# Decode step with gated attention and FFN: the FFN row added inside PSUM, the output copied to one row and stored as one descriptor, and a finer cut of the last weight load

## Chip, cores and metric

The kernel runs on one core of a Trainium2 chip. The metric is the time of one execution on the device in microseconds (us). A run stands for one execution; a comparison is made of several runs of both kernels on the same chip, and the verdict is "faster" or "slower" only beyond 2%. Times inside an execution are read from one profiled execution per kernel and count from the start of its span; the span is some 2 us shorter than the time. PSUM is the memory in which TensorE adds up its products. A transfer (DMA) is issued by an instruction on an engine's queue, moved by up to 16 DMA engines, and has landed when the last update of its semaphore comes; a descriptor is one contiguous run of bytes of it; for the small store each shows as one packet in the trace. The granted clock is the share of TensorE's full clock that the trace records.

## The reference

One token attends over a cache of 32768 positions (32 query heads, 8 key/value heads, head size 128, model width 512), beside a small SwiGLU network, and a scalar gate g mixes both:

```python
g = _sigmoid((x * gate_w).sum(-1, keepdims=True))
a = _A_ref(x, A_k_cache, A_v_cache, A_wq, A_wo)      # softmax(q k) v, then @ wo
b = _B_ref(x, B_w_gate, B_w_up, B_w_down)            # (silu(x w_gate) * (x w_up)) @ w_down
return g * a + (1 - g) * b                           # [1, 1, 512] bf16
```

Keys and values are 134 MB of the 148 MB that the kernel reads, so it is a streaming kernel.

## The kernel before

The sync engine (SP) issues all loads in one order; `wo` is the last, in four pieces with a semaphore each. At the very end it stores the result from four partitions:

```python
WO_CUT = (16, 8, 4, 4)
# ...
elif e[0] == "wo":
    src = A_wo.rearrange("(p j) n -> p j n", j=WOJ)
    j0 = 0
    for c, n in enumerate(WO_CUT):
        sp.dma_start(wo_v[:, j0 : j0 + n, :], src[:, j0 : j0 + n, :]).then_inc(sem_ldo[c], 16)
        j0 += n
# ...
sp.wait_ge(sem_res, 1)
sp.dma_start(out[0, 0, :].rearrange("(c n) -> c n", c=OC), res[0:128:32, :]).then_inc(sem_out, 16)
sp.wait_ge(sem_out, 16)
```

On TensorE (PE) the attention output, brought into 32 columns `O2`, is multiplied with `wo`: 32 steps j, each with four products of one row and 128 columns. The four go to PSUM partitions 0, 32, 64 and 96, so the output row lies in four pieces on four partitions:

```python
pe.wait_ge(sem_O2, 1)
j0 = 0
for c, n in enumerate(WO_CUT):
    pe.wait_ge(sem_ldo[c], 16)
    for j in range(j0, j0 + n):
        for oc in range(OC):                      # OC = 4
            ins = pe.matmul(ps_a[32 * oc : 32 * oc + 1, :], O2[:, j : j + 1],
                            wo_v[:, j, oc * 128 : (oc + 1) * 128],
                            start=(j == 0), stop=(j == WOJ - 1))
    j0 += n
ins.then_inc(sem_pe_a, 1)
```

VectorE (DVE) had computed `(1 - g) * b` about 60 us into the span, and at the end forms the mix in one instruction:

```python
dve.tensor_scalar(b_pre[:, :], ps_b, omg[:, 0:1], None, op0=ALU.mult).then_inc(sem_bpre, 1)
# ... 290 us later ...
dve.wait_ge(sem_pe_a, 1)
dve.scalar_tensor_tensor(res[:, :], ps_a, g_col[:, 0:1], b_pre[:, :], ALU.mult, ALU.add).then_inc(sem_res, 1)
```

## Time and profile before

| | before |
|---|---|
| time, median of 3 runs | 353.69 us (353.55 to 353.71) |
| span of the profiled run | 351.6 us |
| DMA engines busy with loads | 98.3% of the span |
| last piece of `wo` lands | 348.19 us |
| PE ends the last product | 349.03 us |
| store: start of its issue to the end of the span | 349.57 to 351.60, 2.03 us |

The landing is the last update of the load's semaphore in the trace. The page of the kernel before, with the busy share of the DMA engines and their GB/s in 40 slices of the span, and two of the DMA queues (packets, MB, share of 16 engines):

```profile
span 351.6 us, 6018 instructions
...
DMA  8999999999999999999999999999999999999994
GB/s 325 436 406 438 421 440 439 429 427 429 431 432 436 429 429 432 440 425 429 432 440 425 432 429 440 429 429 429 440 432 425 432 436 432 429 429 436 414 418 184
...
q1 hardware_dynamic: 5912, 148.12, 98.3%
q8 instruction: 7, 0.11, 0.1%
```

The DMA engines are at nine tenths or more from the second slice to the last but one. Nothing done faster on another engine in the middle can be seen in the time; only work after the last bytes counts.

The chain of waits of the kernel before, its end (start us, us, what):

```profile
308.15 38.86 DMA ring<-in_A_wo_dram
...
347.05 0.59 PE ps L579 x11
347.64 0.69 issue
348.34 0.71 PE ps L579 x18
...
349.19 0.35 DVE res L821
```

The timeline of the kernel before (start us, length us, engine, line, operation, out<-in, shapes, count, idle time before it):

```profile
343.83 0.19 DVE L817 CAST O<-ps 128x32 bf16<-128x32 f32 x1 [0.30 <-PE ps L570]
...
344.08 2.73 PE L579 MATMUL ps<-ring,O 128*1 128x128 bf16 x96 [0.28 <-DVE O L817]
...
347.05 0.59 PE L579 MATMUL ps<-ring,O 128*1 128x128 bf16 x14 [0.24 <-DMA ring<-in_A_wo_dram]
...
348.34 0.70 PE L579 MATMUL ps<-ring,O 128*1 128x128 bf16 x18 [0.69 <-issue]
349.19 0.35 DVE L821 SCALAR_TENSOR_TENSOR res<-ps,g_col,b_pre 128x128 bf16<-128x128 f32 x1 [5.17 <-PE ps L579]
349.57 0.63 SPq L355 DMA_DIRECT2D out_dram<-res  x1
```

One line of SP's waits (us in total, times, longest us):

```profile
SPq L249 <- DMA out_dram<-res: 1.0, 1, 1.0
```

After the last landing come 0.84 us to the end of PE, 0.54 us until SP has the result (one DVE instruction of 0.35), 0.63 us in which SP issues the store, the wait of 1.0 us for it, and 0.4 us more to the end of the span: 3.4 us in all.

### The profile page before, as it was taken

To read this page: it belongs to the slowest core of one execution; us is meant where nothing else is said; L and a number is where in the kernel's file an instruction comes from. 1 tells how busy PE (TensorE), PEld (TensorE's weight loads), DVE (VectorE), ACT (ScalarE), POOL (GpSimd) and SP (SyncE) were. 2 spreads that over 40 slices of the span, in tenths; PEclk is the share of its full clock that TensorE was granted. 3 is DMA by queue.
4 is the path that set the end of the run, shared out by engine and by line. 5 is a ranking of instruction groups with operands and counts; after the bars stand their busy time and mean duration, and the time that the engine had idled before them with its cause. 6 is when DMAs were issued, how large, how long until landed. Compare 5 with 4: busy or idle time off the path is not lost. (4 is left out here: it accounts for less than half of the span.)

```text
span 351.6 us, 6018 instructions
## 1 busy us (share of the span) xinstructions
PE 252.5 (72%) x2623; PEld 184.6 (53%) x2623; DVE 196.8 (56%) x367; ACT 17.6 (5%) x52; POOL 5.6 (2%) x22
## 2 busy tenths in 40 slices
PE   0159896978395957858495968768497929688755
PEld 0157884745282626546383838455474618475423
DVE  1329276958184845838283756648365917558211
ACT  1000001100100010000100010000100010000100
POOL 0200000000000000000000000000000000000000
PEclk9999679999789998989789698989779987969665
DMA  8999999999999999999999999999999999999994
GB/s 325 436 406 438 421 440 439 429 427 429 431 432 436 429 429 432 440 425 429 432 440 425 432 429 440 429 429 429 440 432 425 432 436 432 429 429 436 414 418 184
DMA packets 5924, 148.24 MB, mean 422 GB/s; under 512 B 666, under 2 KB 668, under 8 KB 924
## 3 DMA queue, kind: packets, MB, share of 16 engines
q1 hardware_dynamic: 5912, 148.12, 98.3%
q8 instruction: 7, 0.11, 0.1%
q14 instruction: 1, 0.01, 0.0%
q10 hardware_dynamic: 4, 0.00, 0.0%
HBM read 148.11 MB, written 0.00 MB: 421 GB/s over the span
## 5 line engine op out<-in xcount | busy, mean ns | idle before, releaser
L736 DVE COPY ktT<-ps 128x1024 bf16<-128x1024 bf16 x256 | 163.3, 685 | 95.5 <-PE ps L446 92.9
L446 PE MATMUL ps<-ident_f,ring 128*128 128x128 f32 x1024 | 158.2, 311 | 56.0 <-PEq L364 56.0
L446 PEld LDWEIGHTS ps<-ident_f,ring 128*128 128x128 f32 x1024 | 133.8, 161 | 89.8 <-issue 65.6
L460 PE MATMUL ps<-ktT,qc 128*32 128x512 bf16 x512 | 41.6, 402 | 15.2 <-DVE ktT L736 15.1
L510 PE MATMUL ps<-ring,ET 128*16 128x512 bf16 x512 | 33.6, 407 | 2.9 <-DMA ring<-in_A_v_cache_dram 2.9
L510 PEld LDWEIGHTS ps<-ring,ET 128*16 128x16 bf16 x512 | 13.3, 92 | 19.3 <-DMA ring<-in_A_v_cache_dram 3.8
L460 PEld LDWEIGHTS ps<-ktT,qc 128*32 128x32 bf16 x512 | 7.9, 95 | 28.1 <-DVE ktT L736 24.3
L741 DVE TENSOR_REDUCE pmaxf<-ps 128x1 f32<-128x512 f32 x16 | 11.1, 692 | 13.7 <-DVEq L740 13.7
L525 PEld LDWEIGHTS ps<-osel,pv_sb 128*128 128x128 f32 x72 | 11.6, 244 | 3.0 <-issue 3.0
L525 PE MATMUL ps<-osel,pv_sb 128*128 128x4 f32 x72 | 11.3, 281 | 1.8 <-PEq L364 1.8
L598 ACT ACTIVATE qc<-qz 128x112 bf16<-128x112 bf16 x8 | 2.4, 296 | 198.6 <-DVE nbias L759 186.5
L614 ACT ACTIVATE P<-ps,nbias 128x512 bf16<-128x512 f32 x16 | 10.7, 675 | 30.2 <-DVE nbias L759 30.1
L772 DVE COPY pv_sb<-ps 128x512 f32<-128x512 f32 x9 | 6.1, 682 | 6.1 <-PE ps L510 6.1
L390 PE MATMUL ps<-xT,ring 128*128 128x1 bf16 x128 | 3.6, 165 | 6.7 <-PEq L364 6.7
L306 POOL PARTITION_ALL_REDUCE gmax<-pmax x8 | 3.0, 372 | 307.4 <-DVE pmax L748 307.4
L492 PE MATMUL ps<-ident,P 128*128 128x128 bf16 x64 | 6.2, 219 | 1.9 <-ACT P L614 1.4
L766 DVE COPY ET<-ps 128x512 bf16<-128x512 bf16 x16 | 6.7, 416 | 1.3 <-PE ps L492 1.3
L415 PEld LDWEIGHTS ps<-xT,ring 128*128 128x128 bf16 x112 | 6.8, 159 | 0.4 <-issue 0.4
L390 PEld LDWEIGHTS ps<-xT,ring 128*128 128x128 bf16 x128 | 3.5, 104 | 6.7 <-issue 6.7
L415 PE MATMUL ps<-xT,ring 128*128 128x1 bf16 x112 | 6.9, 198 | 0.0
L373 PE MATMUL ps<-ones_bf,x_row 1*128 1x1 bf16 x4 | 0.3, 171 | 8.5 <-DMA gw_row<-in_gate_w_dram 8.5
L492 PEld LDWEIGHTS ps<-ident,P 128*128 128x128 bf16 x64 | 4.8, 98 | 2.8 <-ACT P L614 1.9
(71 smaller groups left out, 36.9 us busy)
## 6 DMA issues: line engine op xcount, KB each, us to landing
ring<-in_A_k_cache_dram SPq DMA_DIRECT2D x16, 4096.0 KB, 24.9
ring<-in_A_v_cache_dram SPq DMA_DIRECT2D x15, 4096.0 KB, 32.5
ring<-in_A_wq_dram SPq DMA_DIRECT2D x1, 4096.0 KB, 12.6
ring<-in_A_v_cache_dram SPq DMA_DIRECT2D x2, 2048.0 KB, 29.4
ring<-in_A_wo_dram SPq DMA_DIRECT2D x1, 2048.0 KB, 36.0
ring<-in_B_w_gate_dram SPq DMA_DIRECT2D x1, 1792.0 KB, 26.7
ring<-in_B_w_up_dram SPq DMA_DIRECT2D x1, 1792.0 KB, 30.6
ring<-in_B_w_down_dram SPq DMA_DIRECT2D x1, 1792.0 KB, 43.5
```

What stands on the lines that cost most here:

```text
L390: ins = pe.matmul(ps_m[:, M_Q0 + h : M_Q0 + h + 1], wq_v[:, c, h * DH : (h + 1) * DH], xT[:, c : c + 1], start=(c == 0), stop=(c == KC - 1),)
L415: ins = pe.matmul(ps_m[:, base + j : base + j + 1], wt[:, c, :].rearrange("d (p j) -> d j p", j=FC)[:, j, :], xT[:, c : c + 1], start=(c = ...
L446: ins = pe.transpose(stb[:, t * 64 : (t + 2) * 64], two.bitcast(FP32), ident_f[:, :])
L460: ins = pe.matmul(ps_sc[hf][32 * c : 32 * c + 32, :], qc[:, e, 24 - PB * i : 56 - PB * i], kt[:, e, :], start=(i == 0 and e == 0), stop=(i ...
L492: ins = pe.transpose(ps_pt[:, hf * 512 + m * 128 : hf * 512 + (m + 1) * 128], P[:, hf, m * 128 : (m + 1) * 128], ident[:, :],)
L510: ins = pe.matmul(ps_pv[32 * c : 32 * c + 2 * PB, :], ET[:, hf, col : col + 2 * PB], src[:, i0 : i0 + 2, c, 2 * m : 2 * m + 2, :].rearrang ...
L525: ins = pe.matmul(ps_m[:, M_OT : M_OT + HPG], pv_sb[:, r * DH : (r + 1) * DH], osel[:, r * HPG : (r + 1) * HPG], start=(r == 0), stop=(r = ...
L614: act.activation(P[:, hf, :], ps_sc[hf], ACT.Exp, bias=nbias[:, 0:1], scale=SCALE, accum_out=esum[:, g, hf : hf + 1],).then_inc(sem_exp, 1)
L736: dve.tensor_copy(ktT[:, q % NKT, :], pst[q % NST]).then_inc(sem_cp, 1)
L741: ins = dve.tensor_reduce(pmaxf[:, hf : hf + 1], ps_sc[hf], AX.X, ALU.max)
L766: dve.tensor_copy(ET[:, hf, :], ps_pt[:, hf * 512 : (hf + 1) * 512]).then_inc(sem_ptc, 1)
L772: dve.tensor_copy(pv_sb[:, :], ps_pv).then_inc(sem_pvc, 1)
```

## The change

Its intent is to shorten this tail. The gate is folded into the softmax's denominator (`rSg`), and `(1 - g) * b` is written to one row and added inside PSUM by four products of a single 1 by 1 weight, so that nothing is left after `wo` but a copy. The four pieces are copied to one partition, two by ScalarE (ACT) and two by DVE, so that the store is one descriptor of 1 KB. And `wo` ends in pieces of 2 steps, so that only 8 products are left after the last landing in place of 16. The core of the diff:

```diff
-    WO_CUT = (16, 8, 4, 4)
+    WO_CUT = (16, 8, 4, 2, 2)
@@ SP
-                sp.wait_ge(sem_res, 1)
+                sp.wait_ge(sem_res, OC)
                 sp.dma_start(
-                    out[0, 0, :].rearrange("(c n) -> c n", c=OC), res[0:128:32, :]
+                    out[0, :, :], row[0:1, :]
                 ).then_inc(sem_out, 16)
@@ PE, before the products with wo (ps_a moves from bank 7 to bank 1)
+                for c in range(OC):
+                    pe.matmul(
+                        ps_a[32 * c : 32 * c + 1, :], ones_f[0:1, 0:1],
+                        b_row[0:1, c * 128 : (c + 1) * 128], start=True, stop=False,
+                    )
@@
-                                start=(j == 0),
+                                start=False,
@@ ACT, at the end
+                act.wait_ge(sem_pe_a, 1)
+                for c in range(2):
+                    act.activation(
+                        row[0:1, c * 128 : (c + 1) * 128], ps_a[32 * c : 32 * c + 1, :], ACT.Copy
+                    ).then_inc(sem_res, 1)
@@ DVE, about 60 us into the span: b_pre in one instruction becomes b_row in four
@@ DVE, after the softmax sums
+                dchain(dve.tensor_scalar(rSg[:, :], rS[:, :], g_col[:, 0:1], None, op0=ALU.mult))
@@ DVE, at the end
-                dve.scalar_tensor_tensor(res[:, :], ps_a, g_col[:, 0:1], b_pre[:, :], ALU.mult, ALU.add)
+                for c in range(2, OC):
+                    dve.tensor_copy(
+                        row[0:1, c * 128 : (c + 1) * 128], ps_a[32 * c : 32 * c + 1, :]
+                    ).then_inc(sem_res, 1)
```

More of the change, by code (lines that the diff above doesn't have):

```diff
@@ L201, in bass_gated_mix__gqa_block_cached__swiglu_ffn__decode_kernel @@
         O2 = T("O2", [128, WOJ], BF16)
-        b_pre = T("b_pre", [128, 128], FP32)
-        res = T("res", [128, 128], BF16)
+        b_row = T("b_row", [1, NOUT], FP32)
+        rSg = T("rSg", [128, H], FP32)
+        row = T("row", [1, NOUT], BF16)
         ps = es.enter_context(nc.psum_tensor("ps", [128, 8, 512], FP32))
@@ L221, in bass_gated_mix__gqa_block_cached__swiglu_ffn__decode_kernel @@
         M_BR = 256
-        M_AR = 384
         assert M_O0 + WOJ <= M_BR
         ps_b = ps_m[:, M_BR : M_BR + 128]
-        ps_a = ps_m[:, M_AR : M_AR + 128]
+        ps_a = ps[:, 1, 0:128]
         def slot_of(entry):
@@ L543, in _ @@
                 emit_outb()
-                pe.wait_ge(sem_bpre, 1)
+                pe.wait_ge(sem_bpre, OC)
                 with pe.Fori(1, G):
@@ L572, in _ @@
                 ).then_inc(sem_pe_O2, 1)
+                for c in range(OC):
+                    pe.matmul(
+                        ps_a[32 * c : 32 * c + 1, :],
+                        ones_f[0:1, 0:1],
+                        b_row[0:1, c * 128 : (c + 1) * 128],
+                        start=True,
+                        stop=False,
+                    )
                 pe.wait_ge(sem_O2, 1)
@@ L722, in emit_bpre @@
                     dve.wait_ge(sem_omg, 1)
-                    dve.tensor_scalar(
-                        b_pre[:, :], ps_b, omg[:, 0:1], None, op0=ALU.mult
-                    ).then_inc(sem_bpre, 1)
+                    for c in range(OC):
+                        p = slice(32 * c, 32 * c + 1)
+                        dve.tensor_scalar(
+                            b_row[0:1, c * 128 : (c + 1) * 128],
+                            ps_b[p, :],
+                            omg[p, 0:1],
+                            None,
+                            op0=ALU.mult,
+                        ).then_inc(sem_bpre, 1)
                 def local(k, ins):
@@ L801, in _ @@
                 dve.wait_ge(sem_rS, 1)
+                dve.wait_ge(sem_g, 1)
+                dchain(
+                    dve.tensor_scalar(rSg[:, :], rS[:, :], g_col[:, 0:1], None, op0=ALU.mult)
+                )
                 dve.wait_ge(sem_pe_o, G)
@@ L806, in _ @@
                     dve.tensor_tensor(
-                        oTs[:, 0 : H - HPG], oT[:, 0 : H - HPG], rS[:, 0 : H - HPG], ALU.mult
+                        oTs[:, 0 : H - HPG], oT[:, 0 : H - HPG], rSg[:, 0 : H - HPG], ALU.mult
                     )
@@ L811, in _ @@
                 dve.tensor_tensor(
-                    oTs[:, H - HPG :], ps_m[:, M_OT : M_OT + HPG], rS[:, H - HPG :], ALU.mult
+                    oTs[:, H - HPG :], ps_m[:, M_OT : M_OT + HPG], rSg[:, H - HPG :], ALU.mult
                 ).then_inc(sem_oT1, 1)
@@ L817, in _ @@
                 dve.tensor_copy(O2[:, :], ps_m[:, M_O0 : M_O0 + WOJ]).then_inc(sem_O2, 1)
-                dve.wait_ge(sem_bpre, 1)
-                dve.wait_ge(sem_g, 1)
                 dve.wait_ge(sem_pe_a, 1)
-                dve.scalar_tensor_tensor(
-                    res[:, :],
-                    ps_a,
-                    g_col[:, 0:1],
-                    b_pre[:, :],
-                    ALU.mult,
-                    ALU.add,
-                ).then_inc(sem_res, 1)
+                for c in range(2, OC):
+                    dve.tensor_copy(
+                        row[0:1, c * 128 : (c + 1) * 128], ps_a[32 * c : 32 * c + 1, :]
+                    ).then_inc(sem_res, 1)
 _INS = ['A_x', 'A_k_cache', 'A_v_cache', 'A_wq', 'A_wo', 'B_x', 'B_w_gate', 'B_w_up', 'B_w_down', 'gate_w']
```

## The prediction

> **What bounds it now.** The loads. The page of the kernel before gives the DMA engines 98.3% of the span on queue 1, 148 MB at 422 GB/s, every slice after the first near 430 GB/s except the last (184). PE is busy 72%; its largest idle (56.0 us before the K transposes, ended at L364, the wait for a load) shows that it waits for data. The chain of waits ends: load of wo 308.15 to 347.01, matmuls L579, DVE L821, store. So only what comes after the last bytes can count: about 5 us of 351.6.
>
> **The tail before** (timeline, and issues with landings). The four wo pieces land about 343.2, 345.7, 347.0, 348.2. PE starts wo at 344.08, does 96 products in 2.73 us (28 ns each), idles 0.24 us for piece 3, then 0.69 us ("issue", really piece 4), does the last 18 in 0.71 and ends at 349.05. L821 takes 0.35 (349.19 to 349.54), the store's issue 0.63, and SP waits 1.0 us more for the store; the span ends at 351.6.
>
> **What changes, costed.**
> 1. wo ends in 2+2. After the last landing 8 products remain in place of 16: about 8 x 28 ns = 0.23 us less. The packets halve to 2 KB; the trace's packets take 159 ns at 4 KB and 45 at 1 KB, so I estimate 83 at 2 KB, 16 per engine in place of 8: last landing about 0.06 us later. Net -0.17.
> 2. Four fp32 products of the b row before wo. An fp32 product becomes two PE instructions (L525: 72 for 36; L559: two, 0.40 and 0.42 us at 32 columns; L382 0.35 and 0.37 at one), so roughly 1.6 ns per column each at the low clock (granted 0.50 here). For 128 columns I estimate 0.2 us of array per instruction, eight of them partly overlapped over four column groups: PE starts wo 0.5 to 1.2 us later. PE has 0.24 + 0.69 = 0.93 us of idle time to hide it. I expect 0 to 0.3 us left: centre +0.08.
> 3. L821 (0.35) becomes two copies on each of ACT and DVE in parallel. DVE copies of 32 columns from PSUM take 0.19, so 128 columns about 0.29; ACT 4 columns 0.17, so about 0.28. Two in succession, overlapping a little: about 0.49. Net +0.14.
> 4. The store: one 1 KB descriptor for four of 256 B. Packets 15 ns each become one of about 45; nothing there. Issue 0.63 may shrink (gw_row's one-descriptor issue took 0.21, x_row's, first on its queue, 0.53): -0.1.
> 5. The b row at 59.8 us: one 0.35 us DVE instruction becomes four of about 0.3, so PE's wait at L545 grows by under 1 us. Loads are queued 25 to 43 us ahead (issue to landing), so this is absorbed. The extra multiply rSg (about 0.16 us) lies in DVE's 6.07 us idle before L772: free.
>
> Sum: -0.17 + 0.08 + 0.14 - 0.1 = about -0.05 us. Time: 353.6 us, range 353.1 to 354.1. Faster by over 2%: 0.01, same 0.98, slower 0.01.
>
> **What would show each step.** DMA share and GB/s per slice unchanged. Five wo landings, the last about 348.3. Eight fp32 MATMUL of 1x1 weights near 343.8 to 345; PE idle before the last wo piece smaller than 0.69. PE end about 348.9. Copies end 0.6 us after PE's end. Store issue 0.4 to 0.6.
>
> **What would make it wrong.** fp32 products that run one after another (over 1.3 us) push wo past the landings: up to +0.5 us. Copies across partitions slower than estimated. A store on one engine with a longer receipt. Loads that shift by tenths from run to run.

## The result

The kernel after took 353.09 us (median of 6 runs, 352.64 to 353.33), the kernel before on the same chip 353.62 us (6 runs, 353.45 to 353.86): 0.53 us less, ratio 0.9983 with a 95% interval of 0.9970 to 0.9996. It is "same" by the 2% rule. The prediction said 353.6, with 353.1 as the low end. Ratios here are the mean time of one kernel's runs over that of the other's of the same rounds, so not quite the ratio of the medians that are quoted.

The page of the kernel after, the same lines:

```profile
span 351.3 us, 6042 instructions
...
DMA  8999999999999999999999999999999999999995
GB/s 336 429 399 438 420 442 439 429 423 429 427 440 433 429 422 448 433 425 425 448 418 437 429 433 433 433 429 425 444 433 425 425 448 422 433 429 444 405 422 200
...
q1 hardware_dynamic: 6050, 148.12, 98.4%
q8 instruction: 8, 0.13, 0.2%
```

Share and rate are as before. The chain of waits of the kernel after, its end:

```profile
309.05 39.71 DMA ring<-in_A_wo_dram
...
348.80 0.31 PE ps L587 x8
...
349.14 0.29 DVE row L843
349.43 0.32 DVEq L249
```

The timeline of the kernel after:

```profile
344.49 0.60 PE L574 MATMUL ps<-b_row,ones_f 1*1 1x128 f32 x8
344.60 0.19 DVE L840 CAST O<-ps 128x32 bf16<-128x32 f32 x1 [0.30 <-PE ps L570]
...
345.02 3.49 PE L587 MATMUL ps<-ring,O 128*1 128x128 bf16 x120
...
348.80 0.28 PE L587 MATMUL ps<-ring,O 128*1 128x128 bf16 x8 [0.30 <-DMA ring<-in_A_wo_dram]
349.14 0.56 ACT L637 ACTIVATE row<-ps 1x128 bf16<-1x128 f32 x2 [19.54 <-PE ps L587]
349.14 0.61 DVE L843 CAST row<-ps 1x128 bf16<-1x128 f32 x2 [4.35 <-PE ps L587]
349.78 0.31 SPq L355 DMA_DIRECT2D out_dram<-row  x1
```

And the line of SP's waits of the kernel after:

```profile
SPq L249 <- DMA out_dram<-row: 0.8, 1, 0.8
```

Against before: 120 products run without a gap and the last 8 start 0.04 us after the landing (348.76); the two copies on each engine take 0.56 and 0.61 us; SP's issue takes 0.31 us in place of 0.63; and the wait for the store is 0.8 us in place of 1.0. In this one trace all loads land about 0.5 us later than in before's (last V piece 338.86 against 338.32). That is not the change: already the first load of all, `wq`, landed at 14.02 us against 13.31, before any changed instruction had run. In the 20 traces the last V piece landed between 338.26 and 338.89. So the tail must be counted from the last landing, not from the span's start. This table does so for every kernel (us, from each one's trace; the last column is the sum of the three before it):

| kernel | last landing | landing to PE's end | PE's end to issue | issue to span's end | tail |
|---|---|---|---|---|---|
| before | 348.19 | 0.84 | 0.54 | 2.03 | 3.41 |
| before_rep | 348.23 | 0.54 | 0.53 | 2.03 | 3.10 |
| before_pad | 348.23 | 0.43 | 0.55 | 2.02 | 3.00 |
| e3_before_cut | 348.26 | 0.42 | 0.55 | 2.02 | 2.99 |
| e6_before_store1 | 348.19 | 0.55 | 0.54 | 1.51 | 2.60 |
| after | 348.76 | 0.33 | 0.69 | 1.53 | 2.55 |
| after_rep | 348.38 | 0.42 | 0.69 | 1.52 | 2.63 |
| e1_store4 | 348.19 | 0.33 | 0.69 | 1.52 | 2.54 |
| e2_cut4 | 348.25 | 0.64 | 0.69 | 1.51 | 2.84 |
| e9_store4gap | 348.29 | 0.42 | 0.69 | 2.15 | 3.26 |
| e10_store2gap | 348.70 | 0.33 | 0.68 | 2.10 | 3.11 |
| e7_res_store | 348.28 | 0.33 | 0.37 | 2.02 | 2.72 |
| e4_no_b | 348.18 | 0.60 | 0.68 | 1.52 | 2.80 |
| e4_rep | 348.18 | 0.76 | 0.67 | 1.52 | 2.95 |
| e13_no_b_pad | 348.67 | 0.43 | 0.69 | 1.52 | 2.64 |
| e5_b_x4 | 348.56 | 1.11 | 0.69 | 1.53 | 3.33 |
| e8_cut211 | 348.46 | 0.32 | 0.69 | 1.52 | 2.53 |
| e8_rep | 348.40 | 0.27 | 0.69 | 1.52 | 2.48 |
| e11_act_issue | 348.76 | 0.33 | 0.69 | 1.48 | 2.50 |
| e14_cut211_act | 348.51 | 0.32 | 0.69 | 1.47 | 2.48 |

Columns three and four repeat within hundredths whenever the code is the same. Column two does not: PE's granted clock in the tail was 0.50 in some traces and up to 1.00 in others (windows from 348.0 to 349.2 us: before 0.50, after 0.91, before_rep 1.00, e3 0.50). The Trainium skill, "TensorE: Matmul & The Clock Gate", Part 1, says that the window that decides this runs freely, not in step with the kernel; that fits, and it is noise on this stretch: before and before_rep are the same kernel and differ by 0.30 us.

### The profile page after: what moved, and what is told of

It is laid out like the page before. It is cut to its first block, busy times and chain, and to the rows that moved or that the text cites. A ratio compares the mean times of both kernels' runs of the same rounds, so it can differ in the third digit from the quotient of the medians.

```text
span 351.3 us, 6042 instructions
## 1 busy us (share of the span) xinstructions
PE 252.9 (72%) x2631; PEld 185.8 (53%) x2631; DVE 198.2 (56%) x372; ACT 18.1 (5%) x54; POOL 5.6 (2%) x22
```

## The experiments

The theory at the start (A) was the sum of the two traces: the store gives about 0.5 us, the cut about 0.25, the copies take 0.15 back, the fp32 products are hidden. The rival (B) was that the store is worth nothing and everything comes from the cut. Each kernel was timed in 5 rounds. A kernel was also timed unchanged against itself (before_rep below): its ratio came out at 0.9993 with an interval of 0.998 to 1.0007. The interval reaches 0.48 us to either side, so a difference below about 0.5 us between two kernels is not resolved by the times alone, and the traces have to carry it. The edits below are shortened. The runs came in five calls, each with its own runs of the kernel before; times are best compared within a call.

| call | kernel | time us, median | before in its call | ratio |
|---|---|---|---|---|
| 1 | e1_store4 | 352.94 | 353.71 | 0.9981 |
| 1 | e2_cut4 | 352.97 | 353.71 | 0.9984 |
| 1 | e3_before_cut | 353.50 | 353.71 | 0.9999 |
| 1 | e6_before_store1 | 353.07 | 353.71 | 0.9986 |
| 2 | e9_store4gap | 353.66 | 353.48 | 1.0004 |
| 2 | e4_no_b | 353.21 | 353.48 | 0.9989 |
| 2 | e5_b_x4 | 353.69 | 353.48 | 1.0000 |
| 2 | e7_res_store | 353.41 | 353.48 | 0.9988 |
| 3 | e10_store2gap | 353.26 | 353.79 | 0.9982 |
| 3 | e13_no_b_pad | 352.87 | 353.79 | 0.9970 |
| 3 | e8_cut211 | 352.63 | 353.79 | 0.9965 |
| 3 | e11_act_issue | 353.11 | 353.79 | 0.9971 |
| 4 | after_rep | 352.81 | 353.60 | 0.9983 |
| 4 | e4_rep | 353.22 | 353.60 | 0.9985 |
| 4 | e8_rep | 352.68 | 353.60 | 0.9976 |
| 4 | e14_cut211_act | 352.76 | 353.60 | 0.9974 |
| 5 | before_rep | 353.42 | 353.65 | 0.9993 |
| 5 | before_pad | 353.47 | 353.65 | 0.9999 |

### The store

**e6_before_store1**: the kernel before with a one-descriptor store and nothing else of the change (wrong result, as the edit shows).

```diff
-        res = T("res", [128, 128], BF16)
+        res = T("res", [128, 512], BF16)      # zeroed at the start
-                    out[0, 0, :].rearrange("(c n) -> c n", c=OC), res[0:128:32, :]
+                    out[0, :, :], res[0:1, :]
```

> The kernel before with its store replaced by one descriptor of 1 KB from partition 0 of a wider res (wrong result on purpose: three quarters of the row are zeros). Theory A: issue about 0.3, wait 0.8, time 0.4 to 0.5 us under before, about 353.15. Rival B: no change, 353.6.

Measured: 353.07 us, ratio 0.9986 (0.9972 to 1.0000), 0.64 us under before by the medians. The store's line in the timeline of e6, and its wait:

```profile
349.28 0.32 SPq L355 DMA_DIRECT2D out_dram<-res  x1
```

```profile
SPq L249 <- DMA out_dram<-res: 0.8, 1, 0.8
```

The issue fell to 0.32 us and the wait to 0.8; from the issue's start to the span's end it is 1.51 us in place of 2.03. This one edit gives as much as the whole change. Its interval just touches 1, so it is the trace, with 0.52 us less from issue to end, that rules out rival B.

**e1_store4**: the kernel after, with the store written as four pieces of the same row.

```diff
-                    out[0, :, :], row[0:1, :]
+                    out[0, :, :].rearrange("o (c n) -> o c n", c=OC),
+                    row[0:1, :].rearrange("o (c n) -> o c n", c=OC),
```

> The kernel after, but the row on one partition is stored as four descriptors of 256 B (k of 4) instead of one of 1 KB. Theory A (the store's form pays: issue 0.63 to 0.31 us and wait 1.0 to 0.8 us between the two traces): the issue goes back to about 0.6, the wait to about 1.0, and the time to about 353.55 (0.3 to 0.5 us over the kernel after, so about equal to the kernel before). Rival B (the store is worth nothing, the issue differs by chance or by the source's four partitions, all gain comes from the cut of wo): issue stays about 0.3, time stays about 353.1 (ratio to before 0.998).

Measured: 352.94 us, ratio 0.9981. This experiment failed: its trace shows one packet of 1024 bytes, so the pieces, which lie end to end, had been merged into the same store. It tells nothing of the store, but it is a second sample of the kernel after (issue 0.32 us, 1.52 to the end). Had the packets not been looked at, it would have been taken as proof for rival B.

**e9_store4gap**: the same idea done so that it can't be merged.

```diff
-        row = T("row", [1, NOUT], BF16)
+        row = T("row", [1, 4, 160], BF16)     # copies write row[0:1, c, 0:128]
-                    out[0, :, :], row[0:1, :]
+                    out[0, :, :].rearrange("o (c n) -> o c n", c=4), row[0:1, :, 0:128]
```

> The kernel after, with the row kept on one partition but its four pieces 160 elements apart, so that the store cannot be merged: four descriptors of 256 B from one partition. e1_store4 meant this but its trace shows one packet of 1 KB. Theory A (the number of descriptors or of DMA engines that the store is split over makes it dear): issue 0.6 us, from the issue's start to the end of the span 2.0 us in place of 1.5, time about 353.5. Rival C (the source's four partitions make it dear): issue 0.32, 1.5 us to the end, time 353.0.

Measured: 353.66 us, ratio 1.0004: the gain is gone. The store in the timeline of e9, and its wait:

```profile
349.40 0.75 SPq L355 DMA_DIRECT2D out_dram<-row  x1
```

```profile
SPq L249 <- DMA out_dram<-row: 1.0, 1, 1.0
```

Issue 0.75 us, wait 1.0, 2.15 us to the end, though all bytes come from one partition. So it is not the four partitions (rival C) but the four pieces.

**e10_store2gap**: two pieces of 512 bytes, otherwise as e9.

```diff
-        row = T("row", [1, NOUT], BF16)
+        row = T("row", [1, 2, 288], BF16)
-                    out[0, :, :], row[0:1, :]
+                    out[0, :, :].rearrange("o (c n) -> o c n", c=2), row[0:1, :, 0:256]
```

> The kernel after with the row cut into two pieces with a gap, so two descriptors of 512 B. Theory A1 (cost grows with the number of descriptors): issue and wait lie between those of one and of four: 1.7 to 1.8 us from the issue's start to the span's end (one: 1.52, four: 2.15), time about 353.25. Theory A2 (short descriptors under 512 B are what is dear): as one descriptor, 1.52 us, time 353.0. Theory A3 (anything but a single one is dear): 2.0 us or more, time 353.5.

Measured: 353.26 us, ratio 0.9982; the three other kernels of its call have 0.9965 to 0.9971, so by the ratios it is 0.4 to 0.6 us slower than they are (by the medians 0.15 to 0.63), not clear of noise. The time alone would have fitted A1; the store in the trace decides. The store of e10:

```profile
349.71 0.73 SPq L355 DMA_DIRECT2D out_dram<-row  x1
```

```profile
SPq L249 <- DMA out_dram<-row: 1.0, 1, 1.0
```

Two pieces cost what four do: 0.73 us of issue and 2.10 to the end. A3 holds, A1 and A2 fall. The short length of 256 bytes is not what was dear. What does differ is seen in the packets around the store: the 4-byte packets beside the data are four in before and e9, two in e10, one in after, and after the data the store's semaphore is raised four times, twice and once. The Trainium skill, "DMA: Bandwidth & Descriptors", section "Why a DMA increments its semaphore by 16 and not by 1", says that a transfer is spread over the largest number of engines up to 16 that divides the slowest dimension of both sides, and that each of them posts its own increment. For four and for two pieces that is four and two, and the packets agree; for the single run the packets show one. A store with one such packet took 1.51 to 1.53 us from SP's queue, one with two or four 2.02 to 2.15. The packets' times also show where the half microsecond lies: from the first data packet to the end of the span it is 0.76 to 0.80 us in all 20 traces, with one packet or four, while from the start of SP's issue to that packet it is 0.75 to 0.76 us with one and 1.23 to 1.35 with more. So the cost comes before the first byte of the store moves, not from moving the bytes or from waiting for several engines to finish. In these runs the number of pieces, the number of engines and a pattern of more than one row always went together; no run had several pieces on one engine, so which of them makes the time before the first packet longer is not shown. Why the issue alone doubles, and why it is 0.63 us with the four partitions and 0.73 to 0.75 with the gaps, stays open.

**e7_res_store**: the kernel after, but one DVE copy of all partitions to `res` and the store of before.

```diff
-                for c in range(2, OC):                       # and ACT's two copies go
-                    dve.tensor_copy(row[...], ps_a[...]).then_inc(sem_res, 1)
+                dve.tensor_copy(res[:, :], ps_a).then_inc(sem_res, 1)
-                    out[0, :, :], row[0:1, :]
+                    out[0, 0, :].rearrange("(c n) -> c n", c=OC), res[0:128:32, :]
```

> The kernel after (fp32 sum in PSUM, g folded, new cut) but with one VectorE copy of all 128 partitions and the store of before from four partitions. Theory A: copies 0.29 in place of 0.61 us, store 2.03 in place of 1.52: 0.2 us slower than after, about 353.2, and 0.4 faster than before. Rival (the gain of after lies in the sum and the cut, not the store): faster than after by 0.3, about 352.7.

Measured: 353.41 us, ratio 0.9988. The one copy saves 0.32 us (PE's end to issue 0.37 against 0.69) and the store loses 0.50: the tail is 2.72 us against a mean of 2.57 for the three traces of the kernel after (2.55, 2.63, 2.54). The row is worth its copies, but only just; the times can't show 0.15 us.

### The cut of wo

**e2_cut4**: the kernel after with `WO_CUT = (16, 8, 4, 4)`.

```diff
-    WO_CUT = (16, 8, 4, 2, 2)      # e2, from the kernel after
+    WO_CUT = (16, 8, 4, 4)
-    WO_CUT = (16, 8, 4, 4)         # e3, from the kernel before
+    WO_CUT = (16, 8, 4, 2, 2)
```

What was expected of e2:

> The kernel after with the old cut of wo (16, 8, 4, 4). Theory A: the products after the last landing go from 8 to 16, PE's last stretch from 0.3 to about 0.6 us, time about 353.3 (0.2 to 0.3 us over after, so 0.3 under before). Rival B (all gain from the cut): time equal to before, 353.6.

**e3_before_cut**: the kernel before with `WO_CUT = (16, 8, 4, 2, 2)`.

and for e3:

> The kernel before with the new cut (16, 8, 4, 2, 2) alone. Theory A: 0.2 to 0.3 us under before, about 353.35; last stretch of PE about 0.3 to 0.4 us. Rival B: 353.1, the whole gain. Third: smaller packets land later and give it all back, 353.6.

Measured: e2 352.97 us, 0.9984, beside e1 (which is the kernel after) with 352.94 and 0.9981; e3 353.50 us, 0.9999. In the times the cut is worth 0.0 to 0.2 us, less than theory A expected and not resolved. In the traces it is seen: from the landing to PE's end 0.64 us (e2) against 0.33, 0.33 and 0.42 (e1, after, after_rep), and the last piece lands 9.85 to 9.88 us after the last V piece in the five traces with four pieces and 9.87 to 9.92 in the twelve with five (e2 9.86; e1 9.90, after 9.90, after_rep 9.92), so about 0.03 us is given back. Part of the 0.3 us is the clock's chance, since e2 had 0.50 in its tail and e1 1.00. At like clock the cut is worth less: from the landing to PE's end 16 products took 0.43 us in before_pad and 8 took 0.33 in e1, both at 1.00, and 16 took 0.64 in e2 and 8 took 0.42 in e3, both at 0.50. So the net is about 0.07 to 0.19 us.

### The fp32 products, and a stop that nobody had ordered

**e4_no_b**: the kernel after without the four fp32 products (wrong result).

```diff
-                for c in range(OC):
-                    pe.matmul(ps_a[...], ones_f[0:1, 0:1], b_row[...], start=True, stop=False)
-                                start=False,
+                                start=(j == 0),
```

> The kernel after without its four fp32 products (wrong result on purpose: the FFN part is missing, first wo product starts the sum). Theory A (the products are hidden in PE's wait for the last pieces): PE starts wo about 0.2 us earlier, waits longer for the last piece, last start and end unchanged, time 353.0 within 0.15. Rival (the mode change and the fp32 passes still cost): 0.2 us faster or more, 352.8.

**e5_b_x4**: the products four times over (the first three rounds are overwritten).

```diff
+                for c in [0, 1, 2, 3] * 3:
+                    pe.matmul(ps_a[...], ones_f[0:1, 0:1], b_row[...], start=True, stop=True)
                 for c in range(OC):
                     pe.matmul(ps_a[...], ones_f[0:1, 0:1], b_row[...], start=True, stop=False)
```

> The kernel after with the four fp32 products run four times (first three rounds are overwritten; result right). Theory A: one round costs about 0.17 us of PE's start and more when back to back; three more at 0.25 to 0.4 us each push wo's start by 0.8 to 1.2 us, PE's idle time before the last piece (0.3 us) is used up and 0.5 to 0.9 us shows: about 353.6. Rival (products on 1x1 weights are nearly free): 353.0, idle before the last piece still over 0.1.

Measured: e5 353.69 us, ratio 1.0000. Its products take 1.88 us (344.28 to 346.16) in place of 0.60, so 0.43 for each further round. In its timeline PE then has no gap at all:

```profile
346.09 3.58 PE L595 MATMUL ps<-ring,O 128*1 128x128 bf16 x128
```

PE now ends 1.11 us after the landing in place of 0.33 to 0.42, and 0.7 us show. So one round is hidden and four are not: PE had about 0.3 us to spare (the gap of 0.30 before the last 8 products in the timeline of the kernel after), and one round delays PE by only 0.17 us (from the end of the copy of `O2`, 344.79, to the first product, 345.02, is 0.23; in before 344.02 to 344.08).

e4 missed both expectations: with work taken away it did not get faster but came out at 353.21 us, ratio 0.9989. Its trace shows why: PE stood still for 1.1 us before product 110 of 128 and went on at 348.34, although the piece with products 96 to 111 had landed at 346.93 and the next one at 347.55. This is the "issue" gap of the kernel before with its 14 and 18 products. In every trace with such a stop an instruction packet of queue 8, 16384 bytes, had started on the DMA 2.3 to 2.6 us before PE went on. In before, e6 and e4 the stop lies before product 110; in the kernels with the fp32 products, which make 16 more PE instructions, that is 8 products' worth, it lies before product 102. The Trainium skill, "Runtime: NRT & Kernel Launch", section "Instruction fetch mechanics", says that an engine's instructions come in blocks of 16 KiB, 256 instructions, over a DMA queue, and that this is mostly hidden. The size of the packets and the shift by 16 instructions agree; hidden it is not, here. The traces say one more thing: in all 15 that have such a stop, whether before product 110 or 102, exactly 5339 recorded instructions of PE (weight loads, products and its sequencer's own) come before the product that had to wait. So the stop sits at one place in the instruction stream, whatever the work there is.

**e13_no_b_pad**: e4 with eight cheap bf16 products in the place of the fp32 ones.

```diff
+                for c in [0, 1, 2, 3, 0, 1, 2, 3]:
+                    pe.matmul(ps[32 * c : 32 * c + 1, 2, 0:128], ident[0:1, 0:1], ident[0:1, :],
+                              start=True, stop=True)
```

> e4_no_b (no FFN products, wrong on purpose) with eight bf16 products of one row in their place, so as many PE instructions as the kernel after. In e4_no_b, before and e6 PE stood still before wo product 110 until 2.3 to 2.5 us after a 16 KB instruction packet had started on the DMA; in the kernels with the fp32 products (16 more PE instructions) the stop is before product 102. Theory F (PE waits for its instructions): with the padding the stop is before product 102, ends well before the last piece lands, time 353.0 (e4_no_b 353.21). Rival (the fp32 work or the DMA causes it): stop before product 110 as in e4_no_b, time 353.2.

Measured: 352.87 us, ratio 0.9970, no stop before 110. But none before 102 either, so theory F got the place wrong: here the packet had come at 342.18 us, in the others at 345 to 346, and in no trace with such an early packet did PE stop. Its time came out as theory F had it, but not for theory F's reason.

**e4_rep** and **after_rep**: both unchanged, side by side.

For e4_rep:

> e4_no_b again (no FFN products, wrong on purpose), now beside the kernel after. If the stop before product 110 comes back: 0.15 to 0.3 us slower than after_rep. If the late instruction packet was a chance of that one profile: equal to after_rep within 0.1, the packet before 343 us, and no stop.

For after_rep:

> The kernel after, unchanged, as the yardstick of this call and as one more profile: ratio to before 0.997 to 0.998; from the store's issue to the span's end 1.52 us; stop of PE before product 102, over before the last landing.

Measured: after_rep 352.81 us, 0.9983; e4_rep 353.22 us, 0.9985. The stop came back. The timeline of e4_rep around it, weight loads (PEld) and products (PE):

```profile
346.95 0.20 PEld L579 LDWEIGHTS ps<-ring,O 128*1 128x1 bf16 x14 [0.28 <-DMA ring<-in_A_wo_dram]
348.49 0.26 PEld L579 LDWEIGHTS ps<-ring,O 128*1 128x1 bf16 x18 [1.34 <-issue]
348.49 0.44 PE L579 MATMUL ps<-ring,O 128*1 128x128 bf16 x18 [1.15 <-issue]
```

14 and 18 again, in a cut whose last three pieces have 16, 8 and 8 products, so PE waits for no piece here: the piece with products 112 to 119 had landed at 347.55. From the last landing to PE's end it takes 0.76 us, against 0.42 in after_rep. In means, e4_rep is 0.17 us slower (353.11 against 352.94), not clear of noise.

**before_rep** and **before_pad**: the kernel before once more, and with the same eight bf16 products (e13's added lines) ahead of `wo`.

For before_rep:

> The kernel before, unchanged: ratio 1.000 within 0.001 (that is the noise of these ratios). If the stop is regular: again 14 and 18 products around the last gap, from the last landing to PE's end 0.6 to 0.85 us, an instruction packet at 345.7 to 346.1.

For before_pad:

> The kernel before with eight one-row bf16 products (16 PE instructions, result unused) ahead of wo. Theory F: stop moves from product 110 to 102 or vanishes, the last 16 products start 0.05 us after the landing in place of 0.15: 0.1 us faster than before (353.5), 16 products around the last gap. Rival: nothing moves, stop before 110.

Measured: before_rep 353.42 us, ratio 0.9993; before_pad 353.47 us, 0.9999. In before_rep PE ends 0.54 us after the landing, just under the expected 0.6 to 0.85, at a granted clock of 1.00. The timelines of before_rep and then of before_pad around the last gap:

```profile
347.03 0.20 PEld L579 LDWEIGHTS ps<-ring,O 128*1 128x1 bf16 x14 [0.27 <-DMA ring<-in_A_wo_dram]
348.32 0.26 PEld L579 LDWEIGHTS ps<-ring,O 128*1 128x1 bf16 x18 [1.09 <-issue]
348.32 0.44 PE L579 MATMUL ps<-ring,O 128*1 128x128 bf16 x18 [0.90 <-issue]
```

```profile
347.07 0.31 PEld L587 LDWEIGHTS ps<-ring,O 128*1 128x1 bf16 x16 [0.28 <-DMA ring<-in_A_wo_dram]
348.27 0.21 PEld L587 LDWEIGHTS ps<-ring,O 128*1 128x1 bf16 x16 [0.90 <-DMA ring<-in_A_wo_dram]
348.27 0.39 PE L587 MATMUL ps<-ring,O 128*1 128x128 bf16 x16 [0.61 <-DMA ring<-in_A_wo_dram]
```

In before_rep the stop before product 110 is there again. In before_pad it is gone, the count is 16, the gap's cause is now the load, and the last products start 0.04 us after the landing (348.27 against 348.23) in place of 0.09 to 0.15. So the stop costs the kernel before about 0.1 us, which its time does not resolve.

Over the 20 traces: a stop before product 110 in five (before, before_rep, e6, e4, e4_rep), before 102 in ten (after, after_rep, e1, e2, e7, e8, e8_rep, e9, e10, e11), none in four whose packet came early, at 341.8 to 342.2 us (e3, e13, e14, before_pad), and none in e5, where PE came late to its place. At 102 the stop does no harm, because PE has caught up before the last landing; at 110 it does. What decides between an early and a late packet is not settled: e8 and e14 have the same PE program and differ. That PE was waiting for the instructions is argued from the packets' times, the shift and the common place in the stream; no run took the packet away by itself.

### Can it be faster?

**e8_cut211**, and **e8_rep**, the same kernel beside after_rep:

```diff
-    WO_CUT = (16, 8, 4, 2, 2)
+    WO_CUT = (16, 8, 4, 2, 1, 1)
```

For e8_cut211:

> The kernel after with wo's cut (16, 8, 4, 2, 1, 1), a candidate for a faster one. Theory A: 4 products fewer after the last landing (about 0.1 us), the last landing 0.0 to 0.07 later: 352.95, same within noise. Rival (smaller packets cost): 353.2.

For e8_rep:

> e8_cut211 again beside after. Theory A: 0.05 to 0.1 us faster than after_rep, not clear of noise. Rival (finer pieces help more, as its call suggested): 0.3 us or more faster.

**e11_act_issue**: the store issued from ACT's queue, which then has to wait for DVE's copies only.

```diff
-                sp.wait_ge(sem_res, OC)
-                sp.dma_start(out[0, :, :], row[0:1, :]).then_inc(sem_out, 16)
+                act.wait_ge(sem_res, OC)                     # at the end of ACT's program
+                act.dma_start(out[0, :, :], row[0:1, :]).then_inc(sem_out, 16)
```

> The kernel after with the store issued from ScalarE's queue instead of SyncE's. The one-descriptor issues of this queue took 0.53 us (first) and 0.21 us (second) in the trace. If the issue takes 0.21: 0.1 us faster, 352.9; if 0.5: 0.2 slower, 353.2; the wait after it unchanged (0.8).

**e14_cut211_act**: the edits of e8 and e11 together.

> Both candidates in one: cut (16, 8, 4, 2, 1, 1) and the store issued from ScalarE's queue. Issue 0.23 us, from its start to the span's end 1.48; 0.1 to 0.2 us faster than after_rep.

Measured: e8 352.63 us, 0.9965, and 352.68 us, 0.9976, where after_rep has 352.81 and 0.9983; e11 353.11 us, 0.9971, issue 0.23 us, 1.48 to the end; e14 352.76 us, 0.9974, 1.47 to the end. By the traces the finer cut ends PE 0.27 to 0.32 us after the landing (after 0.33 to 0.42) and lands 0.03 us later (9.94 us after the last V piece); ACT's issue saves 0.04 us. Both candidates point the right way and neither beats the kernel after clear of noise; e14 was expected 0.1 to 0.2 us faster than after_rep and came out 0.05 faster in medians. They do beat the kernel before: e8_rep by 0.9 us in medians.

## Why the prediction was wrong

The direction, the class and the mechanism of a short tail were right; the time fell 0.01 us below the range and the gain of 0.53 us was ten times the 0.05 predicted. Point by point, with the step's terms:

1. **The cut, -0.17.** About right: -0.07 to -0.19 in the traces at like clock, unresolved in the times. The later landing was predicted as 0.06 us and was about 0.03; the 2 KB packets took 84 ns, predicted 83.
2. **The fp32 products, +0.08.** Too pessimistic. The cost was put at 0.5 to 1.2 us of PE's start and was 0.17, because the eight passes overlap (four at a time start 7 ns apart) and 0.30 of their 0.60 us lies before the end of the copy of `O2`, for which PE has to wait in any case. Nothing of it shows. In the two traces without them the tail was even longer (2.80 and 2.95 us against a mean of 2.57), because PE's stop then falls later; the times don't resolve that. The prediction also took the gap of 0.69 us in before for the wait for piece 4. It began two products before that piece, and the count of 14 and 18 said so.
3. **The copies, +0.14.** Right: PE's end to the issue 0.69 us against 0.54, +0.15. Each copy takes 0.27 (ACT) and 0.29 (DVE).
4. **The store, -0.1.** This is the step that failed. "Packets 15 ns each become one of about 45; nothing there" costed the store by its data and gave a little to the issue. Measured: 2.03 us to 1.52, -0.51: issue -0.31, and -0.20 in what follows, nearly all of it (0.60 to 0.43 or 0.45) between the end of the issue and the first packet. The mechanism (a shorter issue) was named, and its size was off by a factor of five with the part after the issue left out. The prediction had the evidence at hand: gw_row's issue with one descriptor took 0.21 us. It weighed that against x_row's 0.53, which was the first on its queue, and took only 0.1.
5. **The b row at 60 us, 0.** Right in effect: DVE's four instructions took 1.48 us in place of 0.35, and PE's idle time there rose by 1.13 us, from 2.20 to 3.33 (predicted: by under 1, so a little too low), all of it absorbed: the DMA share stayed, and the loads of after that were late were late from the first one on.

With the prediction's own terms for the cut and the copies, and the measured ones for the other two, the sum is -0.17 + 0 + 0.14 - 0.51 = -0.54; the measured difference is -0.53. So close an agreement is luck, as the interval of the ratio allows anything from -0.1 to -1.1 us. The traces' tails agree less tightly: 3.41 and 3.10 us in the two traces of before, 2.55, 2.63 and 2.54 in the three of after, so -0.7 in means, of which the clock in the tail is the part that chance moves.

## What to carry to other kernels

A last small store is costed from its issue to its landing, not from its bytes: a row on one partition, stored as one descriptor on one DMA engine, was worth 0.5 us against the same kilobyte in two or four pieces, nearly all of it before the first byte moved, more than it cost to copy the pieces together (0.3 us more than one copy of all partitions). Check in the packets that the store has the form you wrote, as access patterns that lie end to end are merged. And when a timeline's counts around a gap don't fit the program's own grouping, the engine isn't waiting for what you think: look for an instruction packet just before.

## What the Trainium skill lacked or had wrong

- "DMA: Bandwidth & Descriptors" advises using all 16 engines and says nothing of what spreading costs a small store. Here, from SP's queue: issue 0.31 to 0.32 us and 1.51 to 1.53 to the end of the span as one piece on one engine, 0.62 to 0.75 and 2.02 to 2.15 as two or four pieces on as many engines. A one-descriptor issue from ACT's queue took 0.23.
- The same page gives 512 bytes as the length from which transfers run at full rate. That is not wrong, but this store's time did not hang on it: two descriptors of 512 bytes took 2.10 us, four of 256 bytes 2.15.
- "Runtime: NRT & Kernel Launch", "Instruction fetch mechanics", calls the refill of 16 KiB blocks mostly hidden. In 15 of 20 traces PE stood still in straight code (its last branch starts at 321.7 to 324.3 us) until 2.3 to 2.6 us after such a packet had started, by up to 1.4 us between two products; in 4 others the packet came 3 to 4 us earlier and nothing stopped. The page says that the next block is fetched while the current one runs, and not when in it.
- "ScalarE: Activation LUTs" gives, for immediate scale and bias, 186 ns + 0.833 ns per element, which makes 293 ns for 128 elements by our estimate, and an overlap of about 93 ns back to back. The copies of 1 by 128 from PSUM took 267 ns, and the second started 0.29 us after the first, so without overlap.
